# Clustered attention and a gated MLP on one core: POOL's low part of P as one operation of 768 columns, and an order planned with other durations

## The chip, the core and the metric

The kernel runs on one core of a Trainium2 chip. Its engines are PE (TensorE: matmuls, and the weight loads that overlap them), DVE (VectorE), ACT (ScalarE), POOL (GpSimd) and SP (SyncE, which here only issues transfers). Each engine has its own queue of instructions; semaphores join the queues. The metric is the time of one execution on the device, in microseconds (us); lower is better. The profile is of one further execution.

## The reference

Four batches, eight heads, sequence 768, head dimension 64. Each query and each key is assigned to the nearest of 16 normalised centroids of its head, and a query attends only to the keys of its own cluster. The heads' outputs, side by side, go through an MLP with a spatial gate.

```python
q_assign = np.argmax(np.einsum('bhsd,hcd->bhsc', q_n, c_n), axis=-1)
k_assign = np.argmax(np.einsum('bhsd,hcd->bhsc', k_n, c_n), axis=-1)
mask = q_assign[:, :, :, None] == k_assign[:, :, None, :]
scores = np.where(mask, scale * (q @ k.T), -1e9)
attn = softmax(scores)                       # over the keys
x = (attn @ v)                               # heads side by side: 4 x 768 x 512
h = np.maximum(x @ w_in, 0.0)                # 512 -> 1024
u, v = h[..., :512], h[..., 512:]
v_n = (v - mean(v)) / sqrt(var(v) + 1e-6)    # over the 512 features
v_s = einsum('ts,bsd->btd', w_spatial, v_n) + b_spatial[None, :, None]
out = (u * v_s) @ w_out                      # 4 x 768 x 512
```

## The kernel before

Matmul operands are pairs of 16-bit tiles, a high part and a low part (the rest that the high part loses), so that three products stand for one exact product. Much of the work on ACT, DVE and POOL makes these pairs.

Heads are taken two at a time: 16 pairs, four to a batch. For each pair `prep` loads K and Q (tile `raw`) and V (`vraw`), makes high parts on ACT (tile `hq`, L598; `vhl`, L672) and low parts on DVE (`lo`, L604; `vhl`, L677; for the first pairs on POOL, L602 and L675), multiplies by the centroids (L619 to L621) and turns the products into one-hot rows in five DVE operations, the assignment chain (L632 to L637). `shifts` finds, for every query, the largest score of its cluster: for each head 9 groups of matmuls on PE (L733), each followed by a maximum on DVE (L740, tile `nm`); the result goes through a transpose and a row copy on SP's queue (L763, L764) into `hq`.

`attend` handles a head in six tiles of 128 keys by 768 queries. For each tile PE makes the scores (tile `sc`, L784 and L786), ACT takes the exponential into `p` (L790) and casts it to the high part of P (tile `pt`, L792), POOL subtracts for the low part (L796), and PE multiplies both parts by V (54 matmuls, L802). After six tiles DVE divides by the sum (L821 to L823, tile `xn`), ACT and POOL make the pair `xhl` (L825, L826), and SP's queue transposes it (L828, tile `xT`).

`mlp` starts for a batch when its four pairs are there. Six row tiles are projected twice by `w_in` (L847 with `win`): the v half is squashed, measured (L874) and normalised (L887, L888, POOL L889), the u half waits. Then, for each of six tiles, the spatial product (L847 with `wsp`, 18 matmuls), the gate (L908 to L910), a transpose on SP's queue (L911), the product by `w_out` (L847 with `wou`), an eviction on ACT (L918) and the store (L919). The weights themselves are split into high and low parts while the first batches run (L510 on ACT, L523 on DVE; the words of the 64-bit weights are put together by L538 to L540).

No engine's queue is written by hand. `op` records every piece of work with its engine, an estimated duration in us, what it depends on and a key; `Plan.run` then plays the whole program through with these durations and hands out the work in the order in which the engines would come free, the smallest key first. So the estimated durations decide the order on every queue and nothing else: they are not in the built program. `lag`, `OVER` and the rule for the PE clock (matmuls count double where the window before held too few columns) belong to the same estimates.

Around the change the code reads:

```python
for q in range(SPLIT):
    qs = slice(q * S // SPLIT, (q + 1) * S // SPLIT)
    los_.append(op("POOL", 0.04 + 1.64 / SPLIT, lambda ...: G_.tensor_tensor(out=pt.t[:, 1, qs], in0=p32.t[:, qs], in1=pt.t[:, 0, qs], op=ALU.subtract), after=[hi], ...))
o = los_[-1]
prev = op("PE", ..., values, after=[o, prev] + X["v"] + ..., cols=18 * 65, key=AV_KEY)
```

The value products wait for the last piece, so all of the tile's low part has to be there in either form.

Of the kernel before, what the change touches and what calls it, by code (L numbers as in the profile page):

```python
# [15 lines left out]
P = 128  # L16
# [6 lines left out]
X_LOG = 10  # L23
# [12 lines left out]
WINDOW = 10.24 / 3  # L36

# [78 lines left out]
SPLIT = 2  # L116
# [58 lines left out]
OVER = {"PE": 0.0, "ACT": 0.1, "DVE": 0.083, "POOL": 0.04, "SP": 0.0, "NONE": 0.0}  # L175
# [6 lines left out]
class Plan:  # L182
# [25 lines left out]
    def run(self):  # L208
# [19 lines left out]
        hw = [0.0, 0.0]  # L228
# [28 lines left out]
        while done < len(self.ops):  # L257
# [69 lines left out]
def kernel(  # L327
# [117 lines left out]
    def sq():  # L445
        return scratch.t[:, 2 * D + P:3 * D + P]
# [5 lines left out]
    def fill():  # L452
# [13 lines left out]
        (0.1, lambda: V.tensor_tensor(out=sq(), in0=cn(0), in1=cn(0), op=ALU.mult)),  # L466
        (0.1, lambda: V.tensor_reduce(out=ss, in_=sq(), axis=AX.X, op=ALU.add)),
    ], after=[ld_c], use=[scratch], key=KC)
    o = op("POOL", 0.45, lambda: G_.tensor_tensor(out=nrm, in0=ss, in1=half, op=ALU.pow), after=[o, m_half], key=KC)
    o = chain("DVE", [  # L470
        (0.08, lambda: V.tensor_scalar(out=ninv, in0=nrm, scalar1=1e-30, scalar2=None, op0=ALU.max)),
        (0.08, lambda: V.reciprocal(out=ninv, in_=ninv)),
        (0.13, lambda: V.scalar_tensor_tensor(out=nrm, in0=ss, scalar=ninv, in1=nrm, op0=ALU.mult, op1=ALU.add)),
        (0.08, lambda: V.tensor_scalar(out=nrm, in0=nrm, scalar1=0.5, scalar2=1e-6, op0=ALU.mult, op1=ALU.add)),
        (0.08, lambda: V.reciprocal(out=ninv, in_=nrm)),
        (0.2, lambda: V.tensor_scalar(out=cn(0), in0=cn(0), scalar1=ninv, scalar2=C_SCALE, op0=ALU.mult, op1=ALU.mult)),
        (0.1, lambda: V.tensor_copy(out=cn(1), in_=cn(0))),
# [99 lines left out]
    def prep(n):  # L577
# [13 lines left out]
        if n == 0:  # L591
            raws = [move(("SP", "ACT")[h], lambda q, h=h: q.dma_start(out=raw.t[:, h, :], in_=kqT[b, p, :, h, :]), use=[raw] if h else [], new=[] if h else [raw], dma=1.8, key=KP) for h in range(2)]
# [6 lines left out]
        for h, ld in enumerate(raws):  # L599
            if n in LO_POOL:  # L600
                o = op("ACT", 0.83, lambda h=h: A.activation(out=raw.t[:, h, :], in_=raw.t[:, h, :], func=AF.Copy, scale=QK_SCALE), after=[his[h]], use=[raw], key=KL)
                los.append(op("POOL", 1.7, lambda h=h: G_.tensor_tensor(out=lo.t[:, h, :], in0=raw.t[:, h, :], in1=hq.t[:, 0, h, :], op=ALU.subtract), after=[o], use=[raw, hq] + ([lo] if h else []), new=[] if h else [lo], key=KL))  # L602
                continue
            los.append(op("DVE", 0.95, lambda h=h: V.scalar_tensor_tensor(out=lo.t[:, h, :], in0=raw.t[:, h, :], scalar=QK_SCALE, in1=hq.t[:, 0, h, :], op0=ALU.mult, op1=ALU.subtract), after=[his[h]], use=[raw, hq] + ([lo] if h else []), new=[] if h else [lo], key=KL, port=True))  # L604
        if n == 0:
            qa0 = [op("ACT", 0.75, lambda x=x: A.copy(out=hq.t[0:D, x], in_=hq.t[D:P, 0]), after=his, use=[hq], key=KQ) for x in (1, 2)]
# [66 lines left out]
        if n in VL_POOL:  # L673
            o = o_vs = op("ACT", 0.83, lambda: A.activation(out=vraw.t, in_=vraw.t, func=AF.Copy, scale=V_SCALE), after=[o_vh], use=[vraw], key=KV)
            o_vl = op("POOL", 1.7, lambda: G_.tensor_tensor(out=vh.t[:, :, :, D + 2:], in0=vraw.t.rearrange("p t (h d) -> p t h d", d=D), in1=vh.t[:, :, :, 0:D], op=ALU.subtract), after=[o], use=[vraw, vh], key=KV)  # L675
# [42 lines left out]
    def shifts(n):  # L718
# [4 lines left out]
        for h in range(2):  # L723
# [4 lines left out]
            def top(parts, col, n, h=h, nm=nm, tops=tops):  # L728
# [6 lines left out]
                o = op("PE", 0.22, scores, after=X["rows"][h], use=[hq], new=[acc], cols=512, key=K_MX)  # L735
# [31 lines left out]
    def attend(n):  # L767
# [5 lines left out]
        for h in range(2):  # L773
            av = r_acc.new()
            prev = None
            for k in range(NT):
# [11 lines left out]
                o = last["sc"] = op("PE", 0.66, scores, after=X["go"] + [X["shift"][h], last.get("sc")] + exps[-2:-1], use=[hq, lo], new=[sc], cols=2 * S, key=K_SC)  # L788
# [5 lines left out]
                for q in range(SPLIT):  # L794
                    qs = slice(q * S // SPLIT, (q + 1) * S // SPLIT)
                    los_.append(op("POOL", 0.04 + 1.64 / SPLIT, lambda pt=pt, p32=p32, qs=qs: G_.tensor_tensor(out=pt.t[:, 1, qs], in0=p32.t[:, qs], in1=pt.t[:, 0, qs], op=ALU.subtract), after=[hi], use=[p32, pt], key=K_LO))  # L796
# [193 lines left out]
```

## Time and profile before

| what | value |
| --- | --- |
| median of 3 runs | 671.33 us (671.07 to 672.46) |
| the profiled execution, its own time | 671.38 us |
| its span, first to last instruction | 669.6 us |
| mean granted PE clock in it | 0.987 |
| instructions in the span | 16891 |

A row of the stretches gives, for each engine, the time in which it was busy and, in brackets, how many instructions began there. A row of the groups gives line, engine, operation, tiles and shapes, the count, the busy time in us, the mean duration in ns, and behind the second bar the idle time of that engine just ahead of these instructions with what ended it. A row of the waits names who waited for whom: us in total, how often, the longest. A timeline row gives start and duration. Matmuls overlap and their ends are modelled, so PE's busy time is not time at peak rate. "issue" is waiting that the profile doesn't explain.

### The profile page before, as it was taken

How to read it: one execution, taken by the hardware profiler on the slowest of the kernel's cores; microseconds unless marked ns; L12 is line 12 of the kernel's file. 1: busy time of each engine (PE TensorE's matmuls, PEld its weight loads, DVE VectorE, ACT ScalarE, POOL GpSimd, SP SyncE). 2: the span in 40 equal slices, each digit the busy share in tenths (PEclk: the TensorE clock that was granted, in tenths of full speed). 3: DMA queues.
4: the chain of work that ended last, by engine and by line, in shares of the span. 5: the costliest groups of instructions: out<-in, count | busy, mean ns of one | idle time of the engine just before them, and what ended most of it. 6: DMA issues, size and time to landing. Idle time of an engine off the chain costs nothing.

```text
span 669.6 us, 16891 instructions
## 1 busy us (share of the span) xinstructions
PE 629.5 (94%) x6757; PEld 375.9 (56%) x6757; DVE 428.8 (64%) x825; ACT 452.8 (68%) x777; POOL 456.9 (68%) x497
## 2 busy tenths in 40 slices
PE   2799979889999999999999999999999999999996
PEld 1366756556455656656465575666656546544442
DVE  5989999989798974939575475975746511024100
ACT  5579989998796877777584667796849637433121
POOL 2268989999497887768495578896868847613110
PEclk9979979989999999999999999999999999999999
DMA  5468765966634838563622517562401131220223
GB/s 161 135 141 153 158 135 159 216 152 162 152 116 130 197 74 170 100 138 64 133 46 68 125 38 156 137 122 56 92 15 41 25 71 33 66 54 15 49 63 95
DMA packets 105941, 70.51 MB, mean 105 GB/s; under 512 B 90315, under 2 KB 93062, under 8 KB 105862
## 3 DMA queue, kind: packets, MB, share of 16 engines
q1 hardware_dynamic: 102118, 62.74, 42.8%
q10 hardware_dynamic: 3744, 6.69, 3.1%
q8 instruction: 53, 0.87, 0.6%
q14 instruction: 26, 0.21, 0.1%
HBM read 27.63 MB, written 6.29 MB: 51 GB/s over the span
## 4 chain that ended last, share of the span: by engine, by line
PE 58%; DVE 9%; ACT 5%; DMA 4%; issue 2%; POOL 0%; POOLq 0%; ACTq 0%; DVEq 0%
PE acc L847 34%; PE acc L802 9%; PE sc L784 5%; PE sc L786 5%; PE acc L733 4%; DVE nm L740 3%; ACT p L790 2%; DMA out_dram<-o 1%; DVE lo L604 1%; DMA gT<-ghl 1%; ACT pt L792 1%; DMA xT<-xhl 1%; DVE wsp L523 1%; DMA vraw<-in_vp_dram 1%; DVE st L874 1%
## 5 line engine op out<-in xcount | busy, mean ns | idle before, releaser
L796 POOL TENSOR_TENSOR pt<-p,pt 128x384 f16<-128x384 f32 x384 | 355.6, 959 | 48.0 <-issue 20.1
L740 DVE TENSOR_REDUCE nm<-acc 128x1 f32<-128x512 f32 (+1 forms) x288 | 181.8, 680 | 29.3 <-PE acc L733 28.0
L790 ACT ACTIVATE p<-sc 128x768 f32<-128x768 f32 x192 | 152.4, 809 | 23.9 <-PE sc L786 15.3
L792 ACT CAST pt<-p 128x768 f16<-128x768 f32 x192 | 156.7, 833 | 3.5 <-PE acc L802 1.0
L802 PEld LDWEIGHTS <-pt 128*128 128x128 f16 x3456 | 127.1, 98 | 24.5 <-issue 4.3
L802 PE MATMUL acc<-vhl,pt 128*128 128x65 f16 (+1 forms) x3456 | 135.8, 194 | 1.3 <-POOL pt L796 1.1
L847 PE MATMUL acc<-win,xT 128*128 128x512 f16 x576 | 130.2, 379 | 1.0 <-DMA xT<-xhl 0.9
L733 PE MATMUL acc<-hq 80*128 80x256 f16 (+1 forms) x384 | 94.8, 333 | 8.5 <-DVE nm L740 4.2
L784 PE MATMUL sc<-hq,lo 128*128 128x512 f16 (+1 forms) x384 | 95.4, 330 | 7.8 <-ACT p L790 7.1
L847 PE MATMUL acc<-vn,wsp 128*128 128x512 f16 x432 | 96.7, 379 | 0.0
L786 PE MATMUL sc<-hq 81*128 81x512 f16 (+1 forms) x384 | 95.9, 331 | 0.7 <-DVE hq L760 0.7
L847 PEld LDWEIGHTS <-xT 128*128 128x128 f16 x576 | 55.0, 98 | 64.2 <-DMA xT<-xhl 1.4
L908 DVE SCALAR_TENSOR_TENSOR u<-acc,bsp,u 128x512 f32<-128x512 f32 x24 | 17.9, 747 | 95.0 <-PE acc L847 95.0
L847 PEld LDWEIGHTS <-wsp 128*128 128x128 f16 x432 | 41.9, 98 | 49.2
L847 PE MATMUL acc<-wou,gT 128*128 128x512 f16 x288 | 65.8, 379 | 1.8 <-DMA gT<-ghl 1.8
L910 POOL TENSOR_TENSOR ghl<-u,ghl 128x512 f16<-128x512 f32 x24 | 28.2, 1176 | 56.3 <-ACT ghl L909 46.9
L786 PEld LDWEIGHTS <-hq 81*128 81x128 f16 x384 | 37.8, 98 | 27.4 <-issue 2.3
L784 PEld LDWEIGHTS <-lo 128*128 128x128 f16 x384 | 34.5, 98 | 32.7 <-issue 16.5
L909 ACT CAST ghl<-u 128x512 f16<-128x512 f32 x24 | 14.8, 617 | 55.2 <-DVE u L908 36.5
L826 POOL TENSOR_TENSOR xhl<-xn,xhl 128x384 f16<-128x384 f32 x32 | 30.6, 958 | 28.2 <-ACT xhl L825 28.2
L733 PEld LDWEIGHTS <-hq 80*128 80x128 f16 x384 | 32.6, 98 | 27.8 <-issue 9.6
L847 PEld LDWEIGHTS <-gT 128*128 128x128 f16 x288 | 27.9, 97 | 34.2 <-DMA gT<-ghl 2.3
(108 smaller groups left out, 611.7 us busy)
## 6 DMA issues: line engine op xcount, KB each, us to landing
raw<-in_kqT_dram SPq DMA_DIRECT2D x15, 768.0 KB
vraw<-in_vp_dram SPq DMA_DIRECT2D x16, 384.0 KB
out_dram<-o ACTq DMA_DIRECT2D x24, 256.0 KB
hq<-hq SPq DMA_DIRECT2D x15, 384.0 KB
vn<-in_w_in_dram SPq DMA_DIRECT2D x8, 512.0 KB
hq<-lo SPq DMA_DIRECT2D x16, 192.0 KB
lo<-hq SPq DMA_DIRECT2D x16, 192.0 KB
wraw<-in_wsT_dram SPq DMA_DIRECT2D x12, 192.0 KB
```

The source lines that it names most:

```text
L733: T.matmul(out=acc.t[:, c:c + cs.stop - cs.start], lhsT=hq.t[0:R_SH, 1, h, t * P:(t + 1) * P], rhs=hq.t[0:R_SH, 0, h, cs], start=c == 0, s ...
L740: V.tensor_reduce(out=nm.t[:, t, k:k + 1] if n == 1 else nm.t[:, t:t + n, k], in_=src, axis=AX.X, op=ALU.max, negate=True)
L784: T.matmul(out=sc.t[:, cs], lhsT=lo.t[:, h, ks], rhs=hq.t[:, 2, h, cs], start=True, stop=False)
L786: T.matmul(out=sc.t[:, cs], lhsT=hq.t[0:R_E, 0, h, ks], rhs=hq.t[0:R_E, 1, h, cs], start=False, stop=True)
L790: o = op("ACT", 0.81, lambda sc=sc, p32=p32: A.activation(out=p32.t, in_=sc.t[:, 0:S], func=AF.Exp, bias=P_LOG * LN2, scale=SC_UNIT), afte ...
L792: o = op("ACT", 0.83, lambda pt=pt, p32=p32: A.copy(out=pt.t[:, 0, :], in_=p32.t), after=[o], use=[p32], new=[pt], key=K_HI)
L796: los_.append(op("POOL", 0.04 + 1.64 / SPLIT, lambda pt=pt, p32=p32, qs=qs: G_.tensor_tensor(out=pt.t[:, 1, qs], in0=p32.t[:, qs], in1=pt. ...
L802: T.matmul(out=av.t[:, t * (D + 1):t * (D + 1) + w], lhsT=lhsT, rhs=rhs, skip_group_check=True, **f)
L826: xls.append(op("POOL", 1.0, lambda xn=xn, hs=hs: G_.tensor_tensor(out=xhl.t[:, :, 1, hs], in0=xn.t, in1=xhl.t[:, :, 0, hs], op=ALU.subtra ...
L847: T.matmul(out=acc.t, lhsT=lr[m][0], rhs=lr[m][1], start=(m == 0), stop=(m == n - 1))
L908: o = op("DVE", 0.72, lambda: V.scalar_tensor_tensor(out=u32.t, in0=acc.t, scalar=bsp[:, t:t + 1], in1=u32.t, op0=ALU.add, op1=ALU.mult), ...
L910: l = op("POOL", 1.2, lambda: G_.tensor_tensor(out=ghl.t[:, 1, :], in0=u32.t, in1=ghl.t[:, 0, :], op=ALU.subtract), after=[h], use=[u32, g ...
```

## The change

POOL's low part of a tile of P (L796) is one operation of 128x768 in place of two of 128x384. The values that the planner works with change: durations of most pieces of work, the free time behind an ACT operation, the columns below which PE counts as slow, and a first moment ahead of which no transfer lands. Because the planner sets the order, nearly every queue is reordered; no other instruction changes. Two lines are added at the top, so the lines of the program after the change are numbered two higher.

```diff
+BUSY = 3750
+FIRST = 3.05
...
-SPLIT = 2
+SPLIT = 1
...
-OVER = {"PE": 0.0, "ACT": 0.1, "DVE": 0.083, "POOL": 0.04, "SP": 0.0, "NONE": 0.0}
+OVER = {"PE": 0.0, "ACT": 0.108, "DVE": 0.083, "POOL": 0.04, "SP": 0.0, "NONE": 0.0}
...
-        hw = [0.0, 0.0]
+        hw = [0.0, FIRST]
...
-                    if columns.get(k - 1, 0.0) < 3400:
+                    if columns.get(k - 1, 0.0) < BUSY:
...
-                    los_.append(op("POOL", 0.04 + 1.64 / SPLIT, lambda pt=pt, p32=p32, qs=qs: G_.tensor_tensor(out=pt.t[:, 1, qs], in0=p32.t[:, qs], in1=pt.t[:, 0, qs], op=ALU.subtract), after=[hi], use=[p32, pt], key=K_LO))
+                    los_.append(op("POOL", 1.64 if SPLIT == 1 else 0.09 + 1.64 / SPLIT, lambda pt=pt, p32=p32, qs=qs: G_.tensor_tensor(out=pt.t[:, 1, qs], in0=p32.t[:, qs], in1=pt.t[:, 0, qs], op=ALU.subtract), after=[hi], use=[p32, pt], key=K_LO))
...
-            o = op("DVE", 0.08, lambda: V.bn_aggr(out=mv.t[:, k, :], in_=st.t), after=[o], use=[st] + ([mv] if k else []), new=[] if k else [mv], key=0)
+            o = op("DVE", 0.18, lambda: V.bn_aggr(out=mv.t[:, k, :], in_=st.t), after=[o], use=[st] + ([mv] if k else []), new=[] if k else [mv], key=0)
```

The last two lines stand for some thirty others of their kind, in which only the number behind the engine's name differs: among them the casts of the MLP (0.52 to 0.62), POOL's subtractions of 512 columns (1.2 and 1.3 to 1.16), the score tiles on PE (0.66 to 0.648), the value products (0.56 to 0.545) and the projections (0.2135 to 0.217 a matmul).

Three places show what the order makes of it. The first is POOL's queue where head 1 ends, before and after; `p` with its number is the exponential's tile, `xhl` the output pair of the first head.

```order
L796 TENSOR_TENSOR pt<-p_709,pt 128x384 x2
L796 TENSOR_TENSOR pt<-p_750,pt 128x384 x2
L796 TENSOR_TENSOR pt<-p_804,pt 128x384
L826 TENSOR_TENSOR xhl<-xn,xhl 128x6x64
L796 TENSOR_TENSOR pt<-p_804,pt 128x384
L796 TENSOR_TENSOR pt<-p_838,pt 128x384 x2
```

```order
L798 TENSOR_TENSOR pt<-p_720,pt 128x768
L798 TENSOR_TENSOR pt<-p_746,pt 128x768
L828 TENSOR_TENSOR xhl<-xn,xhl 128x6x64
L798 TENSOR_TENSOR pt<-p_774,pt 128x768
L798 TENSOR_TENSOR pt<-p_801,pt 128x768
```

Two halves became one piece; other work of POOL no longer comes between the halves of a tile, and the first head's output stands two tiles earlier.

The second is DVE's queue where the low parts of `wsp` begin, about the ninth and tenth head, before and after.

```order
L874 BN_STATS st<-v_3022 128x6
L821 TENSOR_SCALAR rc<-acc_113 128x6
L875 BN_AGGR mv<-st 128x2
L604 SCALAR_TENSOR_TENSOR lo<-raw,hq 128x768
L677 SCALAR_TENSOR_TENSOR vhl_87<-vraw,vhl_87 128x12x64
L523 SCALAR_TENSOR_TENSOR wsp<-wraw,wsp 128x384 x2
L880 TENSOR_SCALAR a<-mv 128x2
L822 RECIPROCAL rc<-rc 128x6
L823 TENSOR_TENSOR xn<-acc_113,rc 128x384
```

```order
L742 TENSOR_REDUCE nm_89<-acc_112 128x2
L525 SCALAR_TENSOR_TENSOR win<-acc_111,win 128x512
L742 TENSOR_REDUCE nm_89<-acc_113 128x1
L742 TENSOR_REDUCE nm_89<-acc_112 128x1
L525 SCALAR_TENSOR_TENSOR wsp<-wraw,wsp 128x384 x2
L742 TENSOR_REDUCE nm_89<-acc_113 128x2
L742 TENSOR_REDUCE nm_90<-acc_112 128x1
L753 TENSOR_REDUCE nl<-nm_89 128x6
```

Before, the first two low parts come after the statistics of two v tiles, just ahead of the tenth head's division; after, they come among the maxima of the fifth pair, behind the ninth head's division and ahead of any statistics.

The third is PE's queue at the first spatial product (`acc<-vn,wsp`), before and after.

```order
L784 MATMUL sc_108<-hq,lo 128x256
L786 LDWEIGHTS hq
L786 MATMUL sc_108<-hq 128x512
L786 LDWEIGHTS hq
L786 MATMUL sc_108<-hq 128x256
L847 LDWEIGHTS wsp
L847 MATMUL acc_110<-vn,wsp 128x512
```

```order
L735 LDWEIGHTS hq
L735 MATMUL acc_110<-hq 128x256
L735 LDWEIGHTS hq
L735 MATMUL acc_113<-hq 128x512
L849 LDWEIGHTS wsp
L849 MATMUL acc_111<-vn,wsp 128x512
```

Before, the product follows the 75th score tile of the program; after, it follows the 139th group of matmuls for maxima, and nine more score tiles stand ahead of it than before.

More of the change, by code (lines that the diff above doesn't have):

```diff
@@ L591, in prep @@
         if n == 0:
-            raws = [move(("SP", "ACT")[h], lambda q, h=h: q.dma_start(out=raw.t[:, h, :], in_=kqT[b, p, :, h, :]), use=[raw] if h else [], new=[] if h else [raw], dma=1.8, key=KP) for h in range(2)]
+            raws = [move(("SP", "ACT")[h], lambda q, h=h: q.dma_start(out=raw.t[:, h, :], in_=kqT[b, p, :, h, :]), use=[raw] if h else [], new=[] if h else [raw], dma=1.2, key=KP) for h in range(2)]
         else:
@@ L605, in prep @@
         if n == 0:
-            qa0 = [op("ACT", 0.75, lambda x=x: A.copy(out=hq.t[0:D, x], in_=hq.t[D:P, 0]), after=his, use=[hq], key=KQ) for x in (1, 2)]
+            qa0 = [op("ACT", 1.47, lambda x=x: A.copy(out=hq.t[0:D, x], in_=hq.t[D:P, 0]), after=his, use=[hq], key=KQ) for x in (1, 2)]
         else:
@@ L733, in scores @@
                         T.matmul(out=acc.t[:, c:c + cs.stop - cs.start], lhsT=hq.t[0:R_SH, 1, h, t * P:(t + 1) * P], rhs=hq.t[0:R_SH, 0, h, cs], start=c == 0, stop=c > 0 or n == 1, skip_group_check=True)
-                o = op("PE", 0.22, scores, after=X["rows"][h], use=[hq], new=[acc], cols=512, key=K_MX)
+                o = op("PE", 0.2155, scores, after=X["rows"][h], use=[hq], new=[acc], cols=512, key=K_MX)
                 def most():
@@ L867, in v_tile @@
             k = t % 2
-            o = op("ACT", 0.57, lambda: A.activation(out=v32.t, in_=acc.t, func=AF.Relu, scale=2.0 ** -(X_LOG + WIN_LOG)), after=[o], use=[acc], new=[v32], key=K_VT)
+            o = op("ACT", 0.6, lambda: A.activation(out=v32.t, in_=acc.t, func=AF.Relu, scale=2.0 ** -(X_LOG + WIN_LOG)), after=[o], use=[acc], new=[v32], key=K_VT)
             if k == 0:
@@ L897, in u_tile @@
             acc, o = proj(t, 0, pos, (u32,), T_UO)
-            return op("ACT", 0.57, lambda: (u32.alloc(), A.activation(out=u32.t, in_=acc.t, func=AF.Relu, scale=2.0 ** (G_LOG - X_LOG - WIN_LOG - WS_LOG - VN_LOG))), after=[o], use=[acc, u32], key=K_VT)
+            return op("ACT", 0.6, lambda: (u32.alloc(), A.activation(out=u32.t, in_=acc.t, func=AF.Relu, scale=2.0 ** (G_LOG - X_LOG - WIN_LOG - WS_LOG - VN_LOG))), after=[o], use=[acc, u32], key=K_VT)
         gTs = {}
@@ L917, in p_tile @@
             gT.users.append(o)
-            o = op("ACT", 0.57, lambda: A.activation(out=o32.t, in_=acc.t, func=AF.Copy, scale=2.0 ** -(G_LOG + WOUT_LOG)), after=[o], use=[acc], new=[o32], key=T_O)
+            o = op("ACT", 0.6, lambda: A.activation(out=o32.t, in_=acc.t, func=AF.Copy, scale=2.0 ** -(G_LOG + WOUT_LOG)), after=[o], use=[acc], new=[o32], key=T_O)
             op("ACT", 0.06, lambda: A.dma_start(out=out[b, t * P:(t + 1) * P, :], in_=o32.t), after=[o], use=[o32], dma=0.8, key=0)
```

46 lines of the change are left out of this document (23 added, 23 removed).

## The prediction

> **What bounds the kernel now.** I read the engine shares and the forty slices first, then the same execution cut into eight stretches by busy time, then waits and single instructions inside the stretches where PE is not full.
>
> ```profile
> PE 629.5 (94%) x6757; PEld 375.9 (56%) x6757; DVE 428.8 (64%) x825; ACT 452.8 (68%) x777; POOL 456.9 (68%) x497
> PE   2799979889999999999999999999999999999996
> DVE  5989999989798974939575475975746511024100
> POOL 2268989999497887768495578896868847613110
> ```
>
> The mean shares would make PE the bound everywhere. The slices say otherwise: in the first thirteen, DVE and POOL stand at 8 or 9 while PE drops to 7 and 8; after that PE is at 9 to the end. The stretches show how much is open in each (columns: PE, PE weight loads, DVE, ACT, POOL busy, each with its instructions, then the granted clock, DMA share and GB/s).
>
> ```profile
> 0.00:20.00 20.00, 5.86 (x60) 4.04 (x61) 11.66 (x49) 10.72 (x14) 4.44 (x18) 1.00 0.45 143
> 20.00:95.00 75.00, 66.44 (x853) 43.75 (x852) 70.96 (x126) 60.08 (x110) 57.10 (x60) 0.94 0.69 147
> 95.00:145.00 50.00, 43.59 (x666) 30.74 (x664) 46.14 (x83) 46.56 (x80) 46.46 (x51) 0.94 0.71 180
> 145.00:200.00 55.00, 53.20 (x585) 32.02 (x584) 50.55 (x96) 45.99 (x84) 43.36 (x46) 0.98 0.62 144
> 200.00:220.00 20.00, 19.04 (x245) 11.80 (x244) 17.55 (x32) 14.85 (x28) 15.79 (x17) 1.00 0.45 123
> 220.00:580.00 360.00, 357.38 (x3971) 215.81 (x3970) 215.30 (x403) 253.32 (x431) 271.08 (x291) 1.00 0.42 89
> 580.00:650.00 70.00, 70.00 (x326) 31.74 (x325) 15.39 (x41) 17.66 (x30) 16.34 (x16) 1.00 0.23 51
> 650.00:670.00 20.00, 14.01 (x65) 5.99 (x62) 1.23 (x2) 3.62 (x6) 2.31 (x2) 1.00 0.29 79
> ```
>
> From 220 to 650 us PE is busy 427.4 of 430 us at full clock: only 2.6 us can be won there. The last stretch is a chain of product, transpose and store whose instructions stand in the same order in both programs. What a change of POOL and of the order can move lies before 220 us, where PE has little but attention to do and stands still 8.6 us (20 to 95), 6.4 us (95 to 145) and 2.8 us (145 to 220), and runs at 0.94 clock. DVE is the fullest engine there, with POOL and ACT close behind. So the question is when DVE and POOL let PE fill up; all later PE work just follows.
>
> **The change part by part.** (1) POOL's low part of P: 384 operations of 384 columns become 192 of 768. The new form has not run on these tiles, but the same subtraction of 128x768 has, on two others:
>
> ```profile
> L796 POOL TENSOR_TENSOR pt<-p,pt 128x384 f16<-128x384 f32 x384 | 355.6, 959 | 48.0 <-issue 20.1 <-ACT pt L792 16.4 <-POOL pt L796 9.2
> L602 POOL TENSOR_TENSOR lo<-raw,hq 128x768 f16<-128x768 f32 x2 | 3.2, 1638 | 7.5 <-ACT raw L601 7.5
> L675 POOL TENSOR_TENSOR vhl<-vraw,vhl 128x768 f16<-128x768 f32 x2 | 3.2, 1587 | 7.2 <-ACT vraw L674 7.2
> ```
>
> Between 1587 and 1638 ns I take 1620 ns, nearer to L602, whose operands are laid out like P. POOL loses 192 x (2 x 0.959 - 1.62) = 57 us of work. Most of it lies beside a full PE and is worth nothing. It counts where POOL sets the pace:
>
> ```profile
> 95.71 0.54 DVE L823 TENSOR_TENSOR xn<-acc,rc 128x384 f32<-128x384 f32 x1
> 143.83 0.54 DVE L823 TENSOR_TENSOR xn<-acc,rc 128x384 f32<-128x384 f32 x1
> 122.31 11.24 POOL L796 TENSOR_TENSOR pt<-p,pt 128x384 f16<-128x384 f32 x12
> 133.51 0.92 POOL L826 TENSOR_TENSOR xhl<-xn,xhl 128x384 f16<-128x384 f32 x1
> ```
>
> Heads 4 and 8 end at 95.71 and 143.83: 24 score tiles in 48.1 us, 2.00 us each. POOL needs 11.24 / 6 = 1.87 us a tile, plus 0.92 us a head, 2.03 in all: POOL is the pace there. With 1.62 it would need 1.77, 24 x 0.26 = 6.2 us less. But DVE (46.1 of 50 us) and ACT (46.6 of 50) come at once behind it. The order gives way a little: ahead of the end of head 8 DVE now has seven maxima (L740), four operations of an assignment chain and one low part of V fewer; by head 10 the maxima have come back and DVE's list is as long as before. So head 8 may end up to 6 us earlier, and yet at head 10 only that is won which DVE no longer stands still: 75 - 70.96 + 50 - 46.14 = 7.9 us from 20 to 145. The largest named part is maxima waiting for their matmuls, which stand in PE's queue behind value products that wait for POOL (first row 20 to 60 us, second 95 to 145):
>
> ```profile
> DVE nm L740 <- PE acc L733: 2.7, 1, 2.7
> DVE nm L740 <- PE acc L733: 1.9, 2, 1.6
> PE acc L802 <- POOL pt L796: 1.1, 3, 0.6
> ```
>
> Bounds: 0 (the stops have other causes) to -7.9. I take two thirds of the 4.6 us named, **-3.0 us**.
>
> (2) A longer POOL operation can hold up DVE. DVE's subtractions with two SBUF operands take very different times (shortest, median, longest ns; then busy time from 20 to 220 us, rows for L604 and L677):
>
> ```profile
> L604 DVE SCALAR_TENSOR_TENSOR lo<-raw,hq x30: 924/1156/3734, 7.3 to 432.3; 128x768 f16<-128x768 f32 x30
> L677 DVE SCALAR_TENSOR_TENSOR vhl<-vraw,vhl x14: 942/958/1664, 65.5 to 509.4; 128x768 f16<-128x768 f32 x14
> L523 DVE SCALAR_TENSOR_TENSOR wsp<-wraw,wsp x12: 545/670/1236, 169.7 to 203.8; 128x384 f16<-128x384 f32 x12
> 20.00:220.00 200.00, 20.81 (x16) 0.96 0.65 152
> 20.00:220.00 200.00, 5.70 (x5) 0.96 0.65 152
> L523 DVE SCALAR_TENSOR_TENSOR wsp<-wraw,wsp 128x384 f16<-128x384 f32 x12 | 9.2, 775 | 1.6 <-ACT wsp L510 1.6
> ```
>
> Over their shortest forms they lose 20.81 - 16 x 0.924 = 6.0, 5.70 - 5 x 0.942 = 1.0 and 9.2 - 12 x 0.545 = 2.7 us, 9.7 us together, all before 220. The excess goes with POOL's running:
>
> ```profile
> 84.45 5.30 POOL L796 TENSOR_TENSOR pt<-p,pt 128x384 f16<-128x384 f32 x6
> 86.83 3.73 DVE L604 SCALAR_TENSOR_TENSOR lo<-raw,hq 128x768 f16<-128x768 f32 x1
> 93.75 0.95 DVE L604 SCALAR_TENSOR_TENSOR lo<-raw,hq 128x768 f16<-128x768 f32 x1
> ```
>
> The one at 86.83 ends only after POOL's run of six; the one at 93.75 is not held at all. If the loss grows with the length of a POOL operation and shrinks with POOL's share, it becomes 9.7 x (1.62 / 0.959) x (1.77 / 2.03) = 14.3, so +4.6 us on DVE. If it goes with POOL's share alone, 9.7 x 0.87, it is -1.3. I take **+2.0 us**, a little nearer to the upper end, since most excesses (median 1156 against 924) are shorter than one POOL operation.
> [...]
>
> (3) The new durations change the order everywhere up to about the 16th head; behind it the two programs differ in single places. PE's first spatial product (L847 with wsp) has the same ten projections ahead of it as before, but ten maxima groups, nine score tiles and eleven value groups more, and the low parts of wsp come on DVE before these maxima instead of among them. Before, that product and the first projection began here:
>
> ```profile
> 158.69 2.75 PE L847 MATMUL acc<-win,xT 128*128 128x512 f16 x12
> 213.89 4.05 PE L847 MATMUL acc<-vn,wsp 128*128 128x512 f16 x18
> DVE vs L692 <- DMA vraw<-in_vp_dram: 2.7, 1, 2.7
> SPq L528 <- DVE wsp L523: 12.3, 5, 3.3
> ```
>
> From 145 to 220 PE stood still 2.8 us and lost 55 x 0.02 = 1.1 us of clock, 3.9 us. More attention work ahead of the product covers the wait for the normalisation; in exchange each of those maxima is now needed earlier, and DVE is the late engine. Bounds: -3.9 (all covered) to +4.0: DVE's stops of this stretch (2.7 us for a transfer of V, and the other 1.8 of its 4.5 us open between 145 and 200) would fall on PE in full. The loads of wsT move ahead on SP's queue with their users; there five of them waited 12.3 us for a free buffer, and the transposes and row copies queued behind them, on which PE's score tiles depend, waited too. That wait now meets the time of head 9 and 10, and is part of the upper bound. I take **-1.8 us**, nearer to the gain, because the low parts of wsp are out of the way earlier.
>
> (4) The rest at nothing: from 220 on, PE covers any shuffle (bounds -2.6, all that is open, to +2.0, PE's few stops doubled, rounded down); the hand-over of the end is unchanged; the clock's 0.94 before 145 stays, since PE waits for DVE there and matmuls at half speed fill time that is idle anyway.
>
> **Sum:** -3.0 + 2.0 - 1.8 = -2.8 us on the profiled execution of 671.38 (span 669.6), that is 668.6. That execution lies at the median, 671.33. All ends together are -15.7 and +10.6.
>
> **The rivals.**
> Slower: the hold on DVE decides. DVE is busy 95% from 20 to 95 us, so what it loses goes to PE one to one until PE is full. It wins if L604 averages over about 1.65 us (1.31 now). Nothing gained in (1) or (3): 671.4 + 4.6 = 676.0, with (3) against it as well up to 680. For it: the 9.7 us above. Against: POOL has more gaps.
> No change: DVE's list at head 10 is as long as before and its stops return in other places; POOL's 57 us end as idle time. 671.4. For it: DVE 46.1 and ACT 46.6 beside POOL's 46.5.
> Much faster: with POOL out of the way DVE's stops go altogether, -7.9, and -1.8 from (3): 661.7. For it: POOL is full where head 5 to 8 run; against it: only 4.6 us of the stops name the matmuls.
> The change does not do what it says: a 768-column operation costs as much as two halves. Then only (3) is left, 669.6. Against it: both 768-column rows.
>
> **How the numbers follow.** Forecast 0.33 (spread 666 to 670), much faster 0.19, no gain of POOL 0.03, no change 0.18, slower 0.27. Within 0.2% (1.3 us, about what a measurement of this kernel tells from no change) is the no-change case; so faster 0.55, same 0.18, slower 0.27. The range runs from 660 to 677: it leaves about half of the much-faster case's lower side and a third of the slower case, together less than 0.2.
>
> **What would show it.** (1) is right if L796's successor averages near 1.62 us, POOL's busy time falls to about 400 us and DVE stands still less than 7.9 us from 20 to 145. (2): the mean and longest time of L604's successor, 1.4 to 1.5 us expected; over 1.65 the slower rival has it. (3): PE's open time from the first projection to the first spatial product, under 2.8 us. PE's 427 of 430 us after 220 should stand. Wrong I would be, above all, if PE first fills much earlier or later than 160 us, or if the stretch after 220 opened.

## The result, and the profile after

| kernel | median us | lowest to highest | runs |
| --- | --- | --- | --- |
| before | 671.20 | 669.93 to 672.46 | 4 |
| after | 692.54 | 691.88 to 703.42 | 4 |

The ratio of after to before is **1.033** (95% interval 1.0297 to 1.0363): the kernel became 21 us slower, and the prediction (668.6, 660 to 677) was wrong in sign. The profiled execution of after took 703.42 us, 11 us above its median; the section on the experiments shows which piece of its profile is no part of the loss.

First the engine shares and slices of after:

```profile
PE 643.1 (92%) x6757; PEld 380.7 (54%) x6757; DVE 439.8 (63%) x825; ACT 449.9 (64%) x777; POOL 420.6 (60%) x305
PE   2979978877988899999999999799999999999996
DVE  5989999998799955575865475468473820124110
PEclk9989989998999989999999999799999999999999
```

POOL lost 36 us of work (456.9 to 420.6), as meant. But PE, which stood at 9 from the tenth slice on, now is at 7 or 8 in most slices up to the fourteenth (246 us), and there is a new hole in the 26th. The stretches of after (columns as before: PE, PE loads, DVE, ACT, POOL, clock, DMA share, GB/s) say how much is open:

```profile
20.00:95.00 75.00, 63.99 (x834) 42.49 (x833) 70.89 (x114) 57.90 (x106) 52.51 (x33) 0.94 0.63 135
95.00:145.00 50.00, 44.67 (x711) 33.06 (x710) 45.93 (x84) 44.14 (x78) 41.95 (x27) 0.92 0.70 174
145.00:200.00 55.00, 45.18 (x433) 24.51 (x430) 47.35 (x84) 37.19 (x70) 28.71 (x20) 0.94 0.70 167
200.00:220.00 20.00, 17.10 (x227) 11.23 (x227) 20.00 (x33) 18.22 (x29) 17.92 (x12) 1.00 0.33 98
220.00:260.00 40.00, 37.13 (x379) 21.26 (x378) 33.55 (x56) 25.38 (x46) 26.25 (x18) 0.91 0.51 112
260.00:420.00 160.00, 158.70 (x1665) 93.67 (x1664) 99.71 (x189) 106.18 (x187) 97.43 (x69) 1.00 0.40 89
420.00:460.00 40.00, 35.38 (x419) 22.32 (x418) 19.97 (x33) 25.48 (x43) 25.16 (x17) 0.87 0.56 109
460.00:650.00 190.00, 188.83 (x1832) 107.81 (x1829) 86.05 (x185) 114.07 (x192) 116.56 (x86) 1.00 0.27 55
```

For each stretch I add what PE stood open (length less busy) and what its clock lost (length times one less the granted clock), for after and, from the rows of the prediction and one more, for before:

```profile
220.00:260.00 40.00, 40.00 (x452) 23.89 (x451) 30.49 (x51) 29.30 (x52) 33.02 (x34) 1.00 0.67 151
```

From 20 to 145 us that is 24.8 us against 22.5; from 145 to 260 it is 22.5 against 3.9; from 260 to 650, 12.3 against 2.6, of which 9.8 lie between 420 and 460. The three differences, 2.4, 18.6 and 9.7, make 30.7 of the 32.0 us by which the two spans differ (701.6 and 669.6). The main loss sits where the MLP of the first batch begins. The count is a rough one; the experiments repeat it on two further profiles. Two groups of after, and the first projection and the first spatial product of its PE timeline, show the operations that the prediction spoke of:

```profile
L798 POOL TENSOR_TENSOR pt<-p,pt 128x768 f16<-128x768 f32 x192 | 318.9, 1683 | 103.4 <-ACT pt L794 62.1
L606 DVE SCALAR_TENSOR_TENSOR lo<-raw,hq 128x768 f16<-128x768 f32 x30 | 46.8, 1570 | 2.9 <-ACT hq L600 2.9
161.47 2.75 PE L849 MATMUL acc<-win,xT 128*128 128x512 f16 x12
250.00 9.28 PE L849 MATMUL acc<-vn,wsp 128*128 128x512 f16 x36
```

The first projection comes 2.8 us later than before, the first spatial product 36.1 us later (250.00 against 213.89).

### The profile page after: what moved, and what is told of

Read it like the earlier page. It is cut to its first block, busy times and chain, and to the rows that moved or that the text cites. A ratio compares the mean times of both kernels' runs of the same rounds, so it can differ in the third digit from the quotient of the medians.

```text
span 701.6 us, 16696 instructions
## 1 busy us (share of the span) xinstructions
PE 643.1 (92%) x6757; PEld 380.7 (54%) x6757; DVE 439.8 (63%) x825; ACT 449.9 (64%) x777; POOL 420.6 (60%) x305
## 4 chain that ended last, share of the span: by engine, by line
PE 61%; ACT 11%; DVE 11%; issue 7%; DMA 6%; POOL 2%; SPq 1%; POOLq 0%; ACTq 0%; DVEq 0%
PE acc L849 32%; PE acc L804 11%; PE sc L786 6%; PE sc L788 5%; DVE nm L742 5%; PE acc L735 5%; ACT p L792 4%; ACT pt L794 3%; DMA out_dram<-o 2%; DVE lo L606 1%; POOL pt L798 1%; DMA gT<-ghl 1%; DMA wraw<-in_wsT_dram 1%; DMA hq<-oht 1%; DVE xn L825 1%
## 5 line engine op out<-in xcount | busy, mean ns | idle before, releaser
L798 POOL TENSOR_TENSOR pt<-p,pt 128x768 f16<-128x768 f32 x192 | 318.9, 1683 | 103.4 <-ACT pt L794 62.1
L804 PEld LDWEIGHTS <-pt 128*128 128x128 f16 x3456 | 129.1, 99 | 35.8 <-POOL pt L798 11.3
L804 PE MATMUL acc<-vhl,pt 128*128 128x65 f16 (+1 forms) x3456 | 138.9, 195 | 9.6 <-POOL pt L798 9.4
L849 PE MATMUL acc<-win,xT 128*128 128x512 f16 x576 | 132.1, 382 | 0.4 <-DMA xT<-xhl 0.2
L735 PE MATMUL acc<-hq 80*128 80x256 f16 (+1 forms) x384 | 100.7, 351 | 19.5 <-DVE nm L742 11.5
L786 PE MATMUL sc<-hq,lo 128*128 128x512 f16 (+1 forms) x384 | 97.3, 335 | 5.0 <-ACT p L792 4.2
L786 PEld LDWEIGHTS <-lo 128*128 128x128 f16 x384 | 35.8, 100 | 33.0 <-issue 16.5
L606 DVE SCALAR_TENSOR_TENSOR lo<-raw,hq 128x768 f16<-128x768 f32 x30 | 46.8, 1570 | 2.9 <-ACT hq L600 2.9
```

The lines of the kernel that those rows point to most:

```text
L735: T.matmul(out=acc.t[:, c:c + cs.stop - cs.start], lhsT=hq.t[0:R_SH, 1, h, t * P:(t + 1) * P], rhs=hq.t[0:R_SH, 0, h, cs], start=c == 0, s ...
L786: T.matmul(out=sc.t[:, cs], lhsT=lo.t[:, h, ks], rhs=hq.t[:, 2, h, cs], start=True, stop=False)
L798: los_.append(op("POOL", 1.64 if SPLIT == 1 else 0.09 + 1.64 / SPLIT, lambda pt=pt, p32=p32, qs=qs: G_.tensor_tensor(out=pt.t[:, 1, qs], i ...
L804: T.matmul(out=av.t[:, t * (D + 1):t * (D + 1) + w], lhsT=lhsT, rhs=rhs, skip_group_check=True, **f)
L849: T.matmul(out=acc.t, lhsT=lr[m][0], rhs=lr[m][1], start=(m == 0), stop=(m == n - 1))
```

## The experiments

Every time is compared with runs of the kernel before on the same chip; the ratio is this over before, with its 95% interval.

**The operation apart from the order.** The first experiment keeps the order of before and runs the 768-column operation where the second half stood:

```diff
-    ... lambda pt=pt, p32=p32, qs=qs: G_.tensor_tensor(out=pt.t[:, 1, qs], in0=p32.t[:, qs], in1=pt.t[:, 0, qs], op=ALU.subtract) ...
+    ... None if q == 0 else lambda pt=pt, p32=p32: G_.tensor_tensor(out=pt.t[:, 1, :], in0=p32.t, in1=pt.t[:, 0, :], op=ALU.subtract) ...
```

> The kernel of before with its order on every engine; only each pair of POOL operations of 384 columns is one operation of 768, standing where the second half stood. Theory ORDER (the loss lies in the new order, which lets the projections of the first batch run in one piece from 174 to 192 us while POOL and ACT stand idle): 664 to 672 us, at or a little below before, L604's mean stays under 1.5 us. Rival FORM (a POOL operation of 1.68 us holds up DVE and hands the tile to PE in one late piece): 685 to 693 us, L604's mean over 1.55 us, PE waits for POOL's low part over 8 us in all.

The second keeps the order of after and runs two halves one behind the other:

```diff
-    ... lambda pt=pt, p32=p32, qs=qs: G_.tensor_tensor(out=pt.t[:, 1, qs], ...)
+    ... lambda pt=pt, p32=p32: [G_.tensor_tensor(out=pt.t[:, 1, hs], ...) for hs in (slice(0, S // 2), slice(S // 2, S))]
```

> The kernel of after with its order on every engine; only POOL's low part is again two operations of 384 columns, one behind the other. Theory ORDER: 688 to 696 us, no faster than after by more than 0.5%. Rival FORM: 669 to 676 us, near before.

| | two halves | one operation |
| --- | --- | --- |
| order of before | 1 | 1.0053 (1.0032 to 1.0073), 673.27 us |
| order of after | 1.0551 (1.0485 to 1.0616), 705.61 us | 1.033 (1.0297 to 1.0363), 692.54 us |

The order alone costs 5.5%. The single operation wins some 12 us of that back in the new order (after itself took 693.73 us on the chip of this comparison) and costs half a per cent in the old one. Both times lie above what was expected if the order is the cause, by 1 and 10 us, but neither lies where the operation would have put it. So the loss is the order's. The groups and rows of the first experiment that stand for terms (1) and (2), the L604 and L677 rows from 20 to 220 us:

```profile
L796 POOL TENSOR_TENSOR pt<-p,pt 128x768 f16<-128x768 f32 x192 | 322.8, 1702 | 58.8 <-ACT pt L792 33.8 <-PE sc L786 8.4 <-DVE nm L740 4.4
20.00:220.00 200.00, 19.23 (x16) 0.99 0.66 152
20.00:220.00 200.00, 4.97 (x5) 0.99 0.66 152
L523 DVE SCALAR_TENSOR_TENSOR wsp<-wraw,wsp 128x384 f16<-128x384 f32 x12 | 10.6, 894 | 2.0 <-ACT wsp L510 2.0
92.92 0.54 DVE L823 TENSOR_TENSOR xn<-acc,rc 128x384 f32<-128x384 f32 x1
159.49 0.55 DVE L823 TENSOR_TENSOR xn<-acc,rc 128x384 f32<-128x384 f32 x1
```

Over the shortest forms used in the prediction, DVE's subtractions lose 4.4 + 0.3 + 4.1 = 8.8 us, not the 9.7 of before. The fourth head ends 2.8 us earlier than before (92.92 against 95.71). The head of the last row, the ninth, ended at 161.08 before, 1.6 us later than here. Behind the tenth the gain goes: its division stands at 169.45 against 171.04, that of the eleventh at 199.12 against 199.25. The same stretch, in before and in this experiment:

```profile
180.00:200.00 20.00, 19.12 (x195) 11.33 (x194) 19.17 (x40) 18.33 (x33) 17.00 (x18) 1.00 0.44 124
```

```profile
180.00:200.00 20.00, 17.40 (x188) 10.45 (x186) 19.82 (x36) 17.04 (x30) 16.20 (x11) 1.00 0.38 113
```

DVE goes from 19.17 to 19.82 of 20 us and PE loses 1.7 us. I read it so that a full DVE takes back what POOL gave; no run tests that by itself.

**Is it these numbers, or any new plan?** Two more plans, one with before's numbers and a single operation, one that differs from before in one number alone:

```diff
-SPLIT = 2
+SPLIT = 1
```

> The kernel of before planned with all its old numbers and with one POOL operation of 768 columns (the planner counts 1.68 us for it in place of twice 0.86); the order is then a third one, neither that of before nor that of after. Theory ORDER, where the new durations and the rule for the clock do the harm: 664 to 675 us. Rival FORM: 685 to 693 us. A third reading, that any order planned anew from old numbers that had been fitted to one order loses: 675 to 690 us, while the one with one operation in the old order stays at 664 to 672.

```diff
-        hw = [0.0, 0.0]
+        hw = [0.0, 3.05]
```

> The kernel of before, two halves, all its numbers, but one: no transfer is planned to land ahead of 3.05 us (0 before). No duration changes. Theory FITTED (the keys of the order were fitted to the old numbers, and any change of a number that shifts the planned times gives an order some per cent worse): 680 to 705 us. Rival DURATIONS (the new durations and the clock rule do the harm, as they change what the planner thinks dear): 668 to 674 us, since the number moves only the first loads.

They gave 701.75 us, 1.0445 (1.0398 to 1.0491), and 713.68 us, 1.0657 (1.0607 to 1.0707), both slower than every range expected. The second holds the instructions of before, each planned as long as it was, and only the moment ahead of which no transfer lands is different in the plan: 6.6% slower. Three new sets of numbers, three orders that are 3 to 7% slower; the worst comes from the smallest edit. After's numbers are nearer to the trace of before (L875, `bn_aggr`, took 0.177 us; it was planned with 0.08 and is now planned with 0.18); that is no ground to expect a better order.

**The hole between 420 and 460.** After was run again, and once with two buffers for the output tile `o`, whose eviction had waited for a store:

```diff
-        self.t = r.pool.tile(r.shape, r.dtype, name=r.name, bufs=r.bufs)
+        self.t = r.pool.tile(r.shape, r.dtype, name=r.name, bufs=2 if r.name == "o32" else r.bufs)
...
-    id16 = const.tile([P, P], F16, name="id16")
+    id16 = wou[:, 1, NDT - 1, DM - P:DM]
```

> The kernel of after, unchanged, for a second profile. Both theories: 690 to 693 us. If the stop of PE at 440 to 460 us is part of the kernel, it is there again with a granted clock of 0.74 in that stretch; if it was of that one execution, PE is busy over 19 of the 20 us.

> The kernel of after with its order on every engine; the tile of the output product (o) has two buffers on the chip in place of one, so an eviction on ACT no longer waits until the store before it has landed (the planner goes on counting one; the identity matrix of the first 30 us lies in a corner of wou to make room). Theory: the second place of loss, 430 to 450 us, is that wait (ACT stands 5.5 us for two stores, PE 4.7 us behind it, then runs at half clock): 9 us less at most, 683 to 688 us, and the stretch from 420 to 460 us has PE busy over 39 us at clock 1.00. Rival (the wait is only what ends last there, attention is late anyway): 689 to 693 us.

They gave 693.73 us, 1.0337 (1.0317 to 1.0357), and 693.08 us, 1.0337 (1.0308 to 1.0366). Waits of after from 425 to 450 us (who waited for whom, us in total, how often, the longest), three stretches behind them, then the whole place with two buffers:

```profile
ACT o L920 <- DMA out_dram<-o: 5.3, 2, 3.2
PE acc L735 <- ACT o L920: 4.5, 2, 2.9
```

```profile
445.00:450.00 5.00, 2.04 (x8) 0.71 (x7) 1.98 (x3) 2.62 (x5) 0.99 (x1) 0.73 0.62 80
450.00:455.00 5.00, 5.00 (x31) 2.71 (x30) 2.92 (x7) 3.57 (x9) 4.77 (x3) 0.50 0.14 52
455.00:460.00 5.00, 5.00 (x74) 3.94 (x73) 2.76 (x5) 3.46 (x6) 2.59 (x3) 0.74 0.24 45
```

```profile
420.00:460.00 40.00, 39.56 (x521) 25.26 (x518) 29.55 (x49) 30.11 (x53) 30.09 (x19) 1.00 0.68 134
```

With a second buffer the hole is gone from the profile, and the median stays, so the hole is no part of the 21 us. It stands in both profiles of after, whose executions took 703.42 and 699.99 us; no execution of after at its median was profiled, so whether it is there too, where removing it would have won nothing, is not shown. The profiled execution with two buffers took 693.33 us, near the median of after, and keeps the main loss:

```profile
145.00:200.00 55.00, 45.13 (x430) 24.60 (x429) 47.34 (x85) 37.20 (x70) 27.97 (x19) 0.94 0.67 164
200.00:260.00 60.00, 54.58 (x607) 32.69 (x606) 52.88 (x85) 42.94 (x73) 44.15 (x30) 0.94 0.48 107
```

These rows make 22.2 us open or cold from 145 to 260 us, 18.3 more than before, where the first profile of after had 18.6 more and the second has 17.5. The count as a whole is less exact: over all three stretches it explains 16.8 of 21.9 us here and 23.5 of 28.6 in the second profile of after.

**Moving single jobs.** In after, PE's score tiles pause from 161.1 to 187.9 us (158.3 to 174.7 in before), in the time in which the weights `wsp` are loaded and split. Six kernels each changed something in that place. In the short diffs `later` and `sooner` move the chosen jobs, with what depends on them or what they need, in the finished order of after.

```diff
+    at = [was.index(j) for j in jobs[4:]] + [1095, 1110, 1125, 1140]
+    for k in reversed(range(12)):
+        mark = next(o for o in reversed(was[:at[k]]) if o.tag not in ("wsp", "wou"))
+        seq = later(seq, {jobs[k]}, mark)
```

> The kernel of after with one piece of its order moved: the loads, high parts and low parts of wsp are put off by four jobs each, so that none of them stands ahead of the last maximum of head 12 on DVE, ACT or SP; PE's and POOL's order stay word for word. Theory DVE (the low parts of wsp and their wait for a transfer push the maxima of heads 11 and 12 back, and PE has no attention work from 158 to 186 us): the last maximum of head 12 ends about 5 us sooner, the pause of score tiles falls from 28 to about 22 us, the kernel to 684 to 689 us. Rival PE (the pause is PE's own order, 48 projections in a row ahead of head 11's scores): 690 to 694 us, the pause ends where it did.

```diff
+    nl = next(o for o in seq if o.tag == ("nl", 5, 1))
+    tiles = {o for o in seq if o.tag in [("sc", 5, 0, k) for k in range(3)]}
+    return sooner(seq, tiles, seq[seq.index(nl) + 1])
```

The next two have these lines, the first of them beside the edit above, the second alone (there a moved tile may also take another free buffer than the planned one).

> The same, and in addition the first three tiles of head 11 (scores on PE, exponential and cast on ACT, low part on POOL) stand right behind the last maximum of head 12 instead of behind 12 to 48 projections. Theory DVE: 2 to 4 us below the run with wsp moved alone, 681 to 686 us. Rival PE: all the gain comes here: 678 to 686 us against 690 to 694 for the run with wsp moved alone. If neither place matters: 690 to 694 us.

> The kernel of after with one change of order: the first three tiles of head 11 (scores, exponential, cast, low part) stand right behind the last maximum of head 12 instead of behind 12 to 48 projections; DVE and SP keep their order word for word. Theory PE: the pause of score tiles falls from 28 to about 15 us, as before the change, POOL and ACT work under the projections, 682 to 689 us. Rival DVE: what comes after, the next maxima, is late anyway: 690 to 695 us.

```diff
+        raw.t = wouf[:, 768 * (m % 5):768 * (m % 5 + 1)].bitcast(F32)
```

> The kernel of after with its order word for word on every engine; only the loads of wsp go to five buffers (in the memory of wou, which is written later) in place of two, so that they need not wait for the low part of the load two before. Theory WAIT (in the run with wsp moved, DVE stood 16.5 us at wsp's low parts behind ACT's high parts behind the loads, and the kernel lost 21 us; in after the same chain stands 3.4 us on DVE and 8.0 us on ACT, and pushes the maxima of heads 11 and 12 back): these waits fall under 1 us on DVE, the last maximum of head 12 ends 3 to 5 us sooner, 685 to 690 us. Rival PE (the pause of score tiles is PE's own order): 691 to 695 us.

```diff
+    mark = seq[max(i for i, o in enumerate(seq) if o.tag == ("u", 0, 0)) + 1]
+    return sooner(seq, {o for o in seq if o.tag in [("v", 0, 0), ("v", 0, 1)]}, mark)
```

> The kernel of after with one change of order: the 24 matmuls of the first two v tiles and their two evictions on ACT stand right behind the first projection on PE, ahead of the last maxima groups of heads 11 and 12; DVE, POOL and SP keep their order word for word. Theory PE (ready projections are queued behind groups that wait for DVE): PE's 4 us of stops from 160 to 172 us are filled, the stretch keeps full clock, 685 to 690 us. Rival DVE (DVE's list sets when head 11 can begin, PE's order only moves the idle time): 691 to 695 us, the pause of score tiles stays at 28 us.

```diff
-    lo = op("DVE", 0.15 + 0.00104 * n, lambda: V.scalar_tensor_tensor(out=dst()[:, 1, :], in0=x(), scalar=sc, in1=dst()[:, 0, :], op0=ALU.mult, op1=ALU.subtract), ...)
+    if cell == "wsp":
+        low = lambda: (A.activation(out=x(), in_=x(), func=AF.Copy, scale=sc), G_.tensor_tensor(out=dst()[:, 1, :], in0=x(), in1=dst()[:, 0, :], op=ALU.subtract))
...
```

> The kernel of after with its order; only the 12 low parts of wsp are made by POOL in place of DVE, at the same places of the program, with one more scaling on ACT each. POOL stands idle 14 us in that stretch. Theory DVE (DVE's list is what is late; 12 x 0.80 = 9.6 us leave it, 4 of them ahead of head 12's last maximum, and its waits there go as well): 684 to 689 us. Rival PE: 691 to 696 us.

| moved in after | us | ratio | a large wait there, us in total and the longest |
| --- | --- | --- | --- |
| `wsp` four jobs later | 713.8 | 1.0658 (1.0617 to 1.0699) | DVE for ACT's `wsp`, 16.5, 5.3 |
| the same, three score tiles first | 719.2 | 1.0707 (1.0645 to 1.0769) | DVE for ACT's `wsp`, 23.2, 10.0 |
| three score tiles first | 699.65 | 1.0399 (1.0338 to 1.0459) | POOL for the score tile, 12.3, 12.3 |
| five buffers for `wsp`'s loads | 694.48 | 1.0331 (1.0287 to 1.0375) | DVE for ACT's `wsp` as in after, 3.3, 2.8 |
| two v tiles first | 709.87 | 1.058 (1.0504 to 1.0657) | ACT for the projection, 11.9, 9.9 |
| `wsp`'s low parts on POOL | 699.29 | 1.0408 (1.035 to 1.0465) | POOL for ACT, 10.9, 3.3 |

None is faster than after, and but for the one with five buffers each is slower than either range expected of it. The waits of the first (155 to 260 us) and of the one with the v tiles first (155 to 200 us) show what came in place of the old ones:

```profile
ACT wsp L572 <- DMA wraw<-in_wsT_dram: 16.5, 5, 6.6
DVE wsp L585 <- ACT wsp L572: 16.5, 7, 5.3
```

```profile
ACT v L930 <- PE acc L908: 11.9, 2, 9.9
DVE wsp L579 <- ACT wsp L566: 10.0, 3, 7.1
```

I read them so: a job put earlier or later stands in front of others in its engine's queue, and a wait of one engine becomes the wait of the next: transfer, ACT, DVE (16.5 us on ACT, 16.5 on DVE); or product, ACT, transfer's buffer, DVE (11.9 us on ACT, 10.0 on DVE). The kernel with five buffers left the wait that it was to remove in place, so it says nothing on that wait's price.

**Which part of the order costs.** Here the first pieces, of 3135, are handed out by a list, and the planner goes on by itself; the two later kernels take the list from after and go on in before's order:

```diff
+            if len(log) < len(FORCED):
+                o = self.ops[FORCED[len(log)]]
+                e = o.eng
...
+                g = gate(o)
...
+                s = max(g, free[e])
+                pick = (0, o.seq, o)
```

> One POOL operation of 768 columns. The first 1000 of 3135 pieces of work stand in the order of before, word for word (the last of them about 169 us into the program); from there the planner goes on freely with all the numbers of after. Theory BEHIND (the loss comes of what the new order does behind 169 us: more of heads 11 to 14 ahead of the MLP's products): 688 to 698 us, as slow as after, though everything up to 169 us is the old order. Rival AHEAD (the state in which DVE, ACT and PE reach 160 us decides, as the traces at 157 us suggest): 670 to 677 us.

> The same with the first 1400 pieces in the order of before (to about 242 us), then the planner with all the numbers of after. Theory BEHIND, with its place between 169 and 242 us: 671 to 678 us, within 0.5% of the old order with one operation (673.3). If the loss came of the whole program: 680 to 690 us.

> The reverse: the first 1050 pieces in the order of after, word for word (to about 186 us; the pause of score tiles from 158 to 186 us with its 28 us is in it), and all that is left in the order in which before had it. Theory BEHIND: 676 to 684 us, over half of the loss is gone although the pause stays. Rival AHEAD: 688 to 696 us.

> The reverse with the first 1300 pieces in the order of after (to about 233 us). Theory BEHIND, with its place between 186 and 233 us: 688 to 697 us, all of the loss is back. If the place lies behind 233 us: 676 to 684 us.

| order | us | ratio |
| --- | --- | --- |
| before's to 169 us, then planned with after's numbers | 694.04 | 1.0348 (1.0328 to 1.0367) |
| before's to 242 us, then so | 675.58 | 1.007 (1.0043 to 1.0097) |
| after's to 186 us, then before's | 685.89 | 1.0212 (1.0161 to 1.0263) |
| after's to 233 us, then before's | 697.44 | 1.0387 (1.0332 to 1.0442) |

With before's order up to 169 us a loss as large as after's is still there; with it up to 242 us nearly all is gone (the old order with the single operation stands at 1.0053). So in these plans the loss is made between about 170 and 240 us; in after's own order 2.1% are made by 186 us and the rest by 233. The rows of the first two kernels suggest how. All engines from 220 to 260 us, in the first and then in the second:

```profile
220.00:240.00 20.00, 15.12 (x239) 10.53 (x236) 20.00 (x32) 18.34 (x31) 17.25 (x12) 0.88 0.53 136
240.00:260.00 20.00, 17.85 (x75) 7.53 (x74) 11.50 (x19) 3.47 (x9) 5.09 (x5) 0.86 0.50 116
```

```profile
220.00:240.00 20.00, 19.14 (x231) 11.81 (x228) 19.21 (x33) 16.01 (x29) 15.76 (x11) 1.00 0.70 164
240.00:260.00 20.00, 20.00 (x216) 11.76 (x214) 11.38 (x19) 14.21 (x23) 14.56 (x10) 1.00 0.62 140
```

The matmuls of the MLP alone (busy time and count) in the same stretches of the first, then of the second:

```profile
220.00:240.00 20.00, 0.00 (x0) 0.88 0.53 136
240.00:260.00 20.00, 15.19 (x60) 0.86 0.50 116
```

```profile
220.00:240.00 20.00, 7.07 (x32) 1.00 0.70 164
240.00:260.00 20.00, 12.09 (x56) 1.00 0.62 140
```

In the slow order the two kinds of work come in clumps. For 20 us there is attention alone: DVE is full (20.00 of 20), PE waits a quarter of the time and its clock falls to 0.88. Then there is the MLP alone: ACT and POOL are busy 3.47 and 5.09 of 20 us and prepare little for PE. The fast order lays 32 matmuls of the MLP beside the attention, and PE is full. After itself shows the first clump at 200 to 220 us, DVE 20.00 of 20, PE 17.10. The matmuls of the MLP there, in after and then in before:

```profile
200.00:220.00 20.00, 1.68 (x8) 1.00 0.33 98
200.00:220.00 20.00, 10.37 (x47) 1.00 0.45 123
```

The same count over 200 to 220, 220 to 240 and 240 to 260 us parts the profiles of all twenty runs. The six that are at most 2.1% slower than before (before itself, the single operation in the old order, the second and third of this table and the two of the next section) have at least 7.0 us of MLP matmuls in each of these 20 us; each of the fourteen that are 3.3% slower or more has one with 4.0 us or less. That goes together throughout; it isn't a test of the clumps alone.

The third kernel repairs only what follows 186 us. Its rows, which sum to 15.5 us open or cold from 145 to 260 us against after's 22.5:

```profile
145.00:200.00 55.00, 46.45 (x419) 25.11 (x420) 45.59 (x83) 35.94 (x67) 29.29 (x22) 0.91 0.58 137
200.00:220.00 20.00, 19.96 (x275) 13.03 (x273) 15.53 (x33) 12.29 (x25) 12.80 (x9) 0.99 0.33 88
220.00:260.00 40.00, 38.23 (x404) 22.65 (x404) 35.03 (x58) 32.11 (x57) 31.64 (x20) 1.00 0.51 125
```

The pause before 200 us stays (13.5 of these us, 13.1 in after), the rest is repaired, and the ratio falls from about 1.034 to 1.021. That is under two fifths of the loss, where over half was expected, and the interval is wide. So after's loss has two places: the pause, with which 2.1% are left, and the clumps behind it.

**An order for the new durations.** The list was worked out anew, from before's order, for the durations with which after is planned; the instructions are those of after.

> The kernel of after, same instructions, one POOL operation of 768 columns, same durations; the order alone is another: starting from the order of before, single pieces of work were moved forward and back as long as the program with the new durations became shorter by the planner's own count. Theory FITTED (neither the one operation nor the new durations do harm, only an order that no longer fits them): faster than before, 650 to 667 us, PE open less than 10 us from 20 to 220 us (17.8 before), score tiles and MLP products mixed in every stretch of 20 us from 180 us on. Rival MODEL (what the planner counts is too coarse to be fitted to; the old order was good by measurement, not by count): 672 to 695 us.

> The same order with two buffers for o on the chip. If evictions wait for stores in this order too, 1 to 5 us less than with one; if not, equal within 0.3%.

They gave 667.3 us, **0.9962** (0.9935 to 0.9988), and with two buffers for `o` 669.2 us, 0.9977 (0.9944 to 1.001). The instructions of after are thus not slow: in a fitting order they are as fast as before, and by the first one's interval a little faster; the second's includes 1. The expected sign, PE open for less than 10 us from 20 to 220 us, did not come: it is 20.6 us in the first one's profile and 21.1 in the second's, against 17.7 in before. The profiled execution of the first took 671.23 us, 4 us above its median, so its rows can't show where the gain lies. They do show that the mixture is back (all engines, then the matmuls of the MLP alone):

```profile
200.00:220.00 20.00, 19.69 (x231) 11.89 (x230) 19.54 (x37) 16.07 (x30) 13.57 (x9) 1.00 0.67 170
220.00:260.00 40.00, 39.51 (x425) 23.31 (x425) 33.43 (x58) 29.36 (x53) 27.10 (x19) 1.00 0.66 138
```

```profile
200.00:220.00 20.00, 7.10 (x31) 1.00 0.67 170
220.00:240.00 20.00, 10.65 (x48) 1.00 0.80 192
```

## Why the prediction was wrong

**The step that failed is term (3).** It read: "More attention work ahead of the product covers the wait for the normalisation", at -1.8 us, bounds -3.9 to +4.0. Ten maxima groups, nine score tiles and eleven value groups ahead of the first spatial product were counted as cover for PE. The wait was not covered: from 145 to 260 us PE lost 18.6 us more than before, and this in two places. From 145 to 200 us it lost 10.2 us more. There the prediction leaned to the gain "because the low parts of wsp are out of the way earlier"; but while these parts are loaded and split PE's score tiles pause for 27 us, where before they paused for 16. What holds them back stays open, since none of the six changes in that place helped. From 200 to 260 us it lost 8.4 us more. There the work that was counted as cover stands with hardly a matmul of the MLP among it (1.68 us from 200 to 220), DVE is full and PE is open (20.00 and 17.10 of 20 us), and the MLP's matmuls, left for later, run when ACT and POOL have less to do (25.38 and 26.25 of 40 us from 220 to 260, where before had 29.30 and 33.02).

In the term's own stretch, 145 to 220 us, PE stood open 12.7 us where under 2.8 was the sign of being right, and with its clock it lost 12.2 us more than before, three times the upper bound; the 6.5 us from 220 to 260 the prediction had put under (4). The bound, written as +4.0, was taken from DVE's stops of 2.7 and 1.8 us in before, which make 4.5, and these were that small in an order that mixes the two kinds of work. The order showed the pieces moving past the product, and the row of before from 145 to 200 us showed DVE at 50.55 of 55: both were at hand.

**(1), POOL's operation**, had the first half of its mechanism right: heads end earlier. The operation takes 1.68 to 1.70 us, not 1.62, and POOL's busy time came to 420.6 us, not 400. In the old order it wins 2.8 us at the fourth head and 1.6 at the ninth and tenth, against the 3.0 predicted, and the median then shows none of it: 1.0053 (1.0032 to 1.0073). The second half, that DVE's stops shrink, did not come: from 20 to 145 us DVE stood 9.6 us in that order and 8.2 in after, where less than the 7.9 of before was the sign. Part of the gain seems to have gone where the no-change rival put it, to a DVE that is full at 180 to 200 us (PE loses 1.7 us there); another 1.6 us stand open on PE from 420 to 460 us (37.71 busy against 39.30), which nothing here explains. Why the median is half a per cent above before's was not settled.

**(2), the hold on DVE,** was +2.0 predicted. In the old order it is -0.9 (8.8 against 9.7). It doesn't go with the length of POOL's operation: the low parts of K and Q take 39.2 us with halves and 41.2 with one operation in the old order, 47.0 and 46.8 in the new one (42.7 in a second profile of after). The order moves it more than the length does, and so does chance: two executions of after differ by 4.1 us. The prediction's upper estimate, +4.6, let the loss grow with that length; these runs do not agree with it.

**(4)**, nothing behind 220 us, failed at its near end: from 220 to 260 us 6.5 us are open or cold, against a bound of +2.0, and the prediction named an opening there as what would prove it wrong. Behind 260 us it held in the profile with two buffers; the hole at 420 to 460 us costs the median nothing. One reading of the slices was loose without weight for this: PE of before stands at 9 from the tenth slice on, not from the fourteenth.

**The rivals.** Slower came true, but not by the mechanism named. L606 averages 1.57 us, below the 1.65 from which the hold was to decide, and the kernel with before's order up to 169 us has it at 1.30 and is just as slow (1.0348). The rival that was missing is the order itself: that a planner given other numbers makes another mixture. Its price can't be read from a profile of before, but three plans show its size, 3 to 7%. That the order between 170 and 240 us costs is shown by the two kernels whose orders part at 169 us; that it costs by its clumps is read from the rows. The six changes show only that none of them shortens the program; none was made in the clumps.

## What to carry to other kernels

A change of a planner's numbers can be a change of the whole order, as here: take it apart by replaying the old order with the new instructions and the new order with the old ones, before anything is said of either. If the order was found for one set of durations, find it again for the next, from the old order, and don't expect more exact numbers to give a better one by themselves. And when work is moved ahead "as cover", ask which engine sets its pace: here attention almost alone left PE waiting for DVE (2.2 us, and 1.1 for POOL, from 200 to 220 us of after), and every order that was fast had PE's own long products among it, not behind it (at least 7.0 us of them in each 20 us from 200 to 260).

## What the runs showed of the hardware

One DVE subtraction of after took 7.03 us beside four of POOL's operations that followed each other without a gap. POOL's and DVE's timeline of after:

```profile
85.72 6.44 POOL L798 TENSOR_TENSOR pt<-p,pt 128x768 f16<-128x768 f32 x4
85.95 7.03 DVE L606 SCALAR_TENSOR_TENSOR lo<-raw,hq 128x768 f16<-128x768 f32 x1
```

It began 0.23 us into the run of four and ended 0.8 us after it; the shortest of these subtractions takes 0.91 us. That POOL held it is read from the times.

Two of POOL's subtractions of 384 columns take 2 x 0.959 us in before, one of 768 takes 1.70 in the same order. That makes a fixed part of about 0.22 us an instruction, by an estimate that lets the rest grow with the columns.

In after the granted clock stood at 0.50 from 450 to 455 us, behind 5 us in which PE was busy 2.04 us; PE's two waits for ACT's `o` from 425 to 450 us make 4.5 us, the longer 2.9.
